# A four-layer forward and backward pass: where the upper weights are transposed, how the lower pass gets its input, and the order of work at the borders

## The chip, the cores and the metric

The kernel runs on one NeuronCore of one Trainium2 chip. The metric is the device time of one execution in microseconds. The core has a matrix engine (TensorE, PE in the profile, with its weight loads as PEld), three engines for elementwise work (VectorE as DVE, ScalarE as ACT, GpSimd as POOL) and SyncE (SP), from whose queue this kernel issues its transfers to 16 DMA engines. SBUF is the on-chip memory with 128 partitions; PSUM, in 8 banks, takes the results of PE.

## The reference

Four residual layers A, B, A, B with the same weights in both pairs, on x of 2048 tokens by 512 features in bfloat16, each behind a layer norm without affine part; then the gradients of everything for a given gradient of the output.

```python
x = x + A(layernorm(x), wqkv, wo)               # layer 0
x = x + B(layernorm(x), w_gate, w_up, w_down)   # layer 1
x = x + A(layernorm(x), wqkv, wo)               # layer 2
x = x + B(layernorm(x), w_gate, w_up, w_down)   # layer 3
# A: linear attention, 32 heads of 16; phi(t) = where(t > 0, t + 1, exp(t)) + 1e-6
#    kv = sum_s phi(k) v;  z = sum_s phi(k);  o = (phi(q) kv) / (phi(q) z + 1e-6);  o @ wo
# B: (sigmoid(h @ w_gate) * (h @ w_up)) @ w_down, with an inner width F = 1376
out, vjp = jax.vjp(f, x, wqkv, wo, w_gate, w_up, w_down); return out, *vjp(grad_out)
```

## The kernel before

The tokens are cut into 16 tiles of 128 (`NST`), the 512 features into 4 chunks (`NDC`), the inner width into 11 chunks (`NFC`; the last has 96 columns, `FLAST`) and, for PSUM, into three slices of 512, 512 and 352 columns (`FSL`). The residual stream `xs` stays in SBUF in float32. "Upper" weights are w_gate, w_up and w_down of B, "lower" pass means the pass over a B layer that follows its A layer.

The forward work runs in two pairs of layers, 0 with 1 and 2 with 3. For each pair `kq_fwd` walks over the 16 tiles once: it forms the keys and queries (L616), takes the exponential on ACT (`e_t`, L633), clamps it on DVE (`a_t`, L636), joins both to phi (`pk_all`, `pq_all`, L639), stores phi of the query (`sv_phq`, L642) and gathers X, the sum of h transposed times phi(k) (L624). In layer 0 the tile `a_t`, which the clamp writes and the store reads, comes from a pool of three; the forward weights are loaded behind the phq stores of tiles 2, 5, 8 and 11. The queries of the last two tiles are left over (`late_q`); their phi steps are the list `phis`. After the walk, `kq_fwd` makes the small matrix M (L793) and its transpose (L802), and the first tiles of the attention output.

`ab_fwd` is the lower pass. For tile `st` (a step) it does the gate and up products in three slices (`gu`, L922), the sigmoid and its complement on ACT (L924, L926), their product with u on DVE and POOL (`hh_t` at L929, `ssd_t` at L930), and, one or two steps later, the down product (`finish`, L956), which waits for `hhT`, the transpose of `hh_t`. For tiles 2 to 14 (`HH_DMA`) that transpose is one DMA (`dma_T`, L949); for 0, 1 and 15 PE transposes blocks (`t_tp`, L941) and ACT copies them (L944, L946). Beside it the attention output of a later tile passes through `front1` (den), `front2` (`pqnstage`, L863), `front3` (transposes at L374 and the copy to `pqnT`) and `attn_y` (L884, with the residual add at L892 and the statistics at L449 to L455). `ln.apply(st + 2)` then writes the normed `hstage` on ACT (L460), and `ln.stage_T` turns it with four PE transposes (`ln_tp`, L374) and a copy (L381 on DVE or L383 on ACT) into `hT`, the stationary operand of the gate and up products.

The border is the stretch between the two functions: the end of `kq_fwd` (M, attention of tiles 0 and 1, the late phi steps) and steps 0 and 1 of `ab_fwd`, in which nothing but a fixed hand-written order fills PE.

The order of PE, ACT, DVE and POOL in the forward part is as written (a manual schedule). SP is not in it: transfers go out as the program issues them, and a transfer that waits for its data holds those behind it.

The backward pass over B needs the upper weights transposed. `wT_units` makes them during the first pair: nine pieces, each one DMA transpose (two where the last 96 rows of a chunk are left) from the input into a staging tile `wt_st`, and a store from there into DRAM (`wdT_d`, `wuT_d`, `wgT_d`). Two pieces are issued ahead of the border, the others at the even steps of layer 1. `b_weight_loads` loads the three results into the resident tiles at steps 2, 5 and 8 of layer 3, and again for layer 1. The backward passes (`b_bwd_p1`, with `dhh_mm` at L1110, `transposes` at L1209 and L1211 and the product at L1252; `a_bwd_p1`; the weight gradients at L1495 and L1511) follow.

Of the kernel before, what the change touches and what calls it, by code (L numbers as in the profile page):

```python
# [18 lines left out]
D = 512  # L19
# [41 lines left out]
def kernel(  # L61
# [64 lines left out]
    )  # L126
    k.dwp = dict(
# [11 lines left out]
    with tc.tile_pool(name="wfwd", bufs=1, reuse_waits="tile") as wfwd, ExitStack() as lctx, tc.manual_schedule(engines=EM):  # L139
# [25 lines left out]
        def load_wd():  # L165
# [14 lines left out]
            hT=lctx.enter_context(tc.tile_pool(name="ln_hT", bufs=4, reuse_waits="tile")),  # L180
# [3 lines left out]
        with tc.tile_pool(name="aq0", bufs=1, reuse_waits="tile") as aq:  # L184
            A = kq_fwd(k, aq, 0, lns[0], lns[1], x_bf)
            with tc.tile_pool(name="wt_stage", bufs=2, reuse_waits="tile") as wt_stage:
                piece, flush = wT_units(k, wt_stage, B_w_gate, B_w_up, B_w_down)
                piece()
                piece()
                A.tail()  # L190
                ab_fwd(k, A, lns[1], {**{st: piece for st in range(0, 14, 2)}, NST - 2: flush}, nxt=lns[2])
        xctx.close()
        with tc.tile_pool(name="aq2", bufs=1, reuse_waits="tile") as aq:
# [4 lines left out]
            def b_weight_loads():  # L198
                def wd():
                    k.wdT = wb.tile([P, NDC, F], BF16, name="wdT", tag="w_c")  # L200
                    nc.sync.dma_start(out=k.wdT[:], in_=k.wT["wdT"].rearrange("(c p) f -> p c f", p=P))

                def wx(nm, tag):
                    t = wb.tile([P, NFC, D], BF16, name=nm, tag=tag)
                    setattr(k, nm, t)
                    nc.sync.dma_start(out=t[:, 0:NFC - 1, :],
                                      in_=k.wT[nm][0:(NFC - 1) * P, :].rearrange("(c p) j -> p c j", p=P))
                    nc.sync.dma_start(out=t[0:FLAST, NFC - 1, :], in_=k.wT[nm][(NFC - 1) * P:F, :])
                return wd, lambda: wx("wuT", "w_a"), lambda: wx("wgT", "w_b")
# [20 lines left out]
            def last_cb(i):  # L230
# [3 lines left out]
                else:  # L234
                    k.pre["dd"] = pre.tile([P, 2, F], BF16, name="pre_dd")
                    for fs in range(2):
                        dd_ops(k, k.pre["dd"], k.pre["ssd"], fs, dhh_mm(k, k.pre["gT"], fs))
            A.tail()
            ab_fwd(k, A, lns[3], dict(zip((2, 5, 8), b_weight_loads())), out_cb=out_cb, last_cb=last_cb)
# [5 lines left out]
    if True:  # L245
        def load_b_weights():
            wd, wu, wg = b_weight_loads()
            wd()
            wu()
            with tc.issue_after(k.hold):  # L250
                wg()
# [117 lines left out]
def transpose_blocks(k, ps_pool, dst, src_blocks, evac, tag="tp"):  # L369
# [1536 lines left out]
```

## Time and profile before

| | us |
|---|---|
| median of 3 runs | 1136.25 (1135.55 to 1138.84) |
| the profiled execution | 1135.02, span 1133.3 |
| PE busy | 1109.4 (98%) |
| DVE, ACT, POOL busy | 706.9, 484.2, 291.2 |
| DMA, mean over the 16 engines | 90.3% of the span |

Where PE stands by stage (busy us of PE in each stretch, granted clock, share of DMA):

| stretch, us | what runs | PE busy | clock | DMA |
|---|---|---|---|---|
| 18 to 59 | `kq_fwd`, layer 0 | 39.10 of 41 | 1.00 | 0.92 |
| 59 to 88 | border to layer 1, steps 0 to 2 | 22.86 of 29 | 1.00 | 0.70 |
| 88 to 232 | rest of layer 1, walk of layer 2 | 143.30 of 144 | 1.00 | 0.97 |
| 246 to 280 | border to layer 3 | 27.88 of 34 | 1.00 | 0.46 |
| 280 to 398 | rest of layer 3 | 118.00 of 118 | 1.00 | 0.91 |
| 398 to 1133 | backward | 731.10 of 735 | 1.00 | 0.94 |

How to read it: a line of the work list has the start, the duration, the engine, the program line, the operation, output<-input by the program's names, shapes and count; in brackets stands how long the engine had been idle before, and what ended that. The duration of a group of pipelined products reaches into the next group. SPq is SP issuing a transfer, not the transfer itself.

### The profile page before, as it was taken

How to read it: one execution, taken by the hardware profiler on the slowest of the kernel's cores; microseconds unless marked ns; L12 is line 12 of the kernel's file. 1: busy time of each engine (PE TensorE's matmuls, PEld its weight loads, DVE VectorE, ACT ScalarE, POOL GpSimd, SP SyncE). 2: the span in 40 equal slices, each digit the busy share in tenths (PEclk: the TensorE clock that was granted, in tenths of full speed). 3: DMA queues.
4: the chain of work that ended last, by engine and by line, in shares of the span. 5: the costliest groups of instructions: out<-in, count | busy, mean ns of one | idle time of the engine just before them, and what ended most of it. 6: DMA issues, size and time to landing. Idle time of an engine off the chain costs nothing.

```text
span 1133.3 us, 20011 instructions
## 1 busy us (share of the span) xinstructions
PE 1109.4 (98%) x7468; PEld 648.8 (57%) x7468; DVE 706.9 (62%) x1344; ACT 484.2 (43%) x909; POOL 291.2 (26%) x518
## 2 busy tenths in 40 slices
PE   8979999998999999999999999999999999999998
PEld 4444554444555555554456468855546745448888
DVE  6788886778776456664975850166664976852211
ACT  6676666555756543433625431224324515410000
POOL 5647776435666400000110220000000110210000
PEclk9999999999999999999999999999999999999999
DMA  8967999855899999997899997799998899969996
GB/s 270 309 197 212 273 282 283 245 142 183 223 294 265 269 261 262 302 255 207 222 244 313 220 260 237 195 283 289 257 283 260 205 282 289 241 194 298 263 205 192
DMA packets 413682, 282.36 MB, mean 249 GB/s; under 512 B 198608, under 2 KB 399504, under 8 KB 409744
## 3 DMA queue, kind: packets, MB, share of 16 engines
q1 hardware_dynamic: 412432, 280.03, 90.3%
q8 instruction: 58, 0.95, 0.3%
q10 hardware_dynamic: 1152, 1.05, 0.3%
q14 instruction: 40, 0.33, 0.1%
HBM read 125.44 MB, written 115.70 MB: 213 GB/s over the span
## 4 chain that ended last, share of the span: by engine, by line
PE 89%; DVE 6%; DMA 3%; ACT 1%; issue 1%; POOL 0%; DVEq 0%; SPq 0%; POOLq 0%
PE p_ps L1511 18%; PE dh_ps L1252 13%; PE dh_ps L1756 7%; PE p_ps L1495 7%; PE y_ps L956 6%; PE dhh_ps L1110 6%; PE g_ps L922 6%; PE u_ps L922 6%; PE T_ps L1209 3%; PE dpk_ps L1791 2%; PE GT_ps L1652 2%; PE dp_ps L1624 2%; PE y_ps L884 2%; PE t_mm L616 2%; PE X_ps L624 2%; PE t_ps L374 1%
## 5 line engine op out<-in xcount | busy, mean ns | idle before, releaser
L1511 PE MATMUL p_ps<-p_set,p_a 128*128 128x256 bf16 (+1 forms) x2032 | 210.1, 264 | 0.0
L1511 PEld LDWEIGHTS <-p_a 128*128 128x128 bf16 x2048 | 185.9, 98 | 22.2
L1132 DVE TENSOR_TENSOR dd<-dhh_ps,ssd 128x512 bf16<-128x512 f32 x144 | 82.4, 629 | 121.3 <-PE dhh_ps L1110 117.4
L930 POOL TENSOR_TENSOR ssd_t<-hh_t,oms 128x512 bf16<-128x512 bf16 (+1 forms) x96 | 100.7, 1060 | 50.1 <-ACT out_t L226 13.5
L1252 PEld LDWEIGHTS <-ddT 128*128 128x128 bf16 (+1 forms) x704 | 67.6, 98 | 74.6 <-DMA ddT<-dd 2.4
L922 PEld LDWEIGHTS <-hT 128*128 128x128 bf16 x768 | 72.5, 98 | 65.2 <-DVE hT L381 1.4
L1084 POOL TENSOR_SCALAR ab<-c 128x2 f32<-128x2 f32 x64 | 12.4, 194 | 377.9 <-DVE junk L1081 364.7
L1211 ACT COPY ddT<-T_ps 128x1024 bf16<-128x1024 bf16 (+1 forms) x72 | 58.8, 819 | 115.2 <-PE T_ps L1209 62.0
L1076 ACT ACTIVATE t_sb<-dh_ps,rstd_all 128x512 f32<-128x512 f32 x64 | 44.0, 688 | 115.7 <-issue 65.0
L922 PE MATMUL g_ps<-wg,hT 128*128 128x512 bf16 (+1 forms) x384 | 90.0, 357 | 0.4 <-DVE hT L381 0.4
L924 ACT ACTIVATE ssd_t<-g_ps 128x512 bf16<-128x512 f32 (+1 forms) x96 | 53.4, 556 | 86.1 <-PE g_ps L922 80.3
L922 PE MATMUL u_ps<-wu,hT 128*128 128x512 bf16 (+1 forms) x384 | 90.0, 357 | 0.0
L1485 DVE TENSOR_TENSOR dw_stg<-p_ps,dw_stg 128x512 bf16<-128x512 f32 (+3 forms) x43 | 28.1, 653 | 98.1 <-PE p_ps L1511 81.4
L929 DVE TENSOR_TENSOR hh_t<-u_ps,ssd_t 128x512 bf16<-128x512 f32 (+1 forms) x96 | 60.4, 631 | 44.0 <-PE u_ps L922 34.2
L1252 PE MATMUL dh_ps<-wgT,ddT 128*128 128x512 bf16 (+1 forms) x352 | 85.2, 379 | 0.0
L1252 PE MATMUL dh_ps<-wuT,ddT 128*128 128x512 bf16 (+1 forms) x352 | 81.3, 379 | 0.8 <-DMA ddT<-dd 0.7
L956 PE MATMUL y_ps<-wd,hhT 128*128 128x512 bf16 (+1 forms) x352 | 81.3, 379 | 0.6 <-DVE x L958 0.6
L1495 PE MATMUL p_ps<-p_a,p_set 128*128 128x512 bf16 (+1 forms) x352 | 81.2, 379 | 0.0
L1110 PE MATMUL dhh_ps<-wdT,gTb 128*128 128x512 bf16 x336 | 74.2, 357 | 0.0
L956 PEld LDWEIGHTS <-hhT 128*128 128x128 bf16 (+1 forms) x352 | 34.2, 98 | 41.1 <-issue 0.7
L1081 DVE SCALAR_TENSOR_TENSOR junk<-t_sb,h_ld 128x512 bf16<-128x512 f32 x48 | 37.2, 774 | 28.9 <-ACT t_sb L1076 23.7
L926 ACT ACTIVATE oms<-g_ps 128x512 bf16<-128x512 f32 (+1 forms) x96 | 52.8, 550 | 3.9 <-POOL ssd_t L930 3.7
(227 smaller groups left out, 1824.2 us busy)
## 6 DMA issues: line engine op xcount, KB each, us to landing
p_set<-sv_hdd SPq DMA_DIRECT2D x30, 1024.0 KB, 6.2
sv_ssd<-ssd_t SPq DMA_DIRECT2D x32, 688.0 KB, 4.2
ssd<-sv_ssd SPq DMA_DIRECT2D x24, 688.0 KB, 5.1
sv_hdd<-dd SPq DMA_DIRECT2D x24, 512.0 KB, 5.0
sv_hdd<-hh_t SPq DMA_DIRECT2D x32, 320.0 KB, 4.4
p_a<-sv_h SPq DMA_DIRECT2D x16, 512.0 KB, 6.5
p_set<-sv_dqk SPq DMA_DIRECT2D x8, 1024.0 KB, 7.5
h_ld<-sv_h SPq DMA_DIRECT2D x24, 256.0 KB, 4.7
```

What stands on the lines that cost most here:

```text
L922: nc.tensor.matmul(ps[:, 0:w], lhsT=hT[:, kc, :], rhs=w_sb[:, kc, c0:c0 + w], start=(kc == 0), stop=(kc == NDC - 1))
L924: nc.scalar.activation(ssd_t[:, 0, c0:c0 + w], g_ps[:, 0:w], ACT.Sigmoid)
L929: nc.vector.tensor_tensor(hh_t[:, c0:c0 + w], u_ps[:, 0:w], ssd_t[:, 0, c0:c0 + w], ALU.mult)
L930: nc.gpsimd.tensor_tensor(ssd_t[:, 1, c0:c0 + w], hh_t[:, c0:c0 + w], oms[:, 0:w], ALU.mult)
L956: nc.tensor.matmul(y_ps[:], lhsT=T["hhT"][0:r, fc, :], rhs=k.wd[0:r, fc, :], start=(fc == 0), stop=(fc == NFC - 1))
L1110: k.nc.tensor.matmul(ps[:, 0:w], lhsT=gT[:, jc, :], rhs=k.wdT[:, jc, c0:c0 + w], start=(jc == 0), stop=(jc == NDC - 1))
L1132: k.nc.vector.tensor_tensor(dd_part(dd, a, fs), ps[:, 0:w], ssd[:, a, c0:c0 + w], ALU.mult)
L1211: nc.scalar.copy(out[:, :, 0:nfull, :], tps[:, :, 0:nfull, :])
L1252: nc.tensor.matmul(T["dh"][:], lhsT=T["ddT"][0:r, dd_block(a, fc), :], rhs=(k.wuT, k.wgT)[a][0:r, fc, :], start=(i == 0), stop=(i == 2 * N ...
L1495: nc.tensor.matmul(ps[0:r, :], lhsT=set_t[:, st, c * P:c * P + r], rhs=self.ops[j["l"], "g"][:, st, :], start=(st == 0), stop=(st == NST - 1))
L1511: nc.tensor.matmul(ps[:, icl * w:(icl + 1) * w], lhsT=self.ops[j["l"], "h"][:, st, ic * P:(ic + 1) * P], rhs=set_t[:, st, 0:w], start=(st ...
L1756: nc.tensor.matmul(dh_ps[:], lhsT=lhsT, rhs=rhs, start=(i == 0), stop=(i == len(ops) - 1))
```

## The change

- *Upper weights.* `wT_units` and its staging are gone from the first pair. In the second pair the same pieces are transposed straight into the resident tiles (`k.bw`): four ahead of the border, two, two and one after the stores of steps 0, 1 and 2. The last chunk is transposed as the last 128 columns, overlapping the one before, and its first 32 rows are set to zero (`zero_rows`, step 6). At steps 7, 9 and 11 the resident tiles are stored to DRAM, from where layer 1's backward pass loads them with one transfer each.
- *Input of the lower pass.* In layer 1 the `hT` of tiles 3 to 15 is made by a DMA transpose of `hstage`, issued after `ln.apply` two steps ahead of its use. Layer 3 keeps PE transposes. The pools of `hT` and `pqnT` lose one buffer each.
- *Borders* (both pairs). 24 and 14 transposes of the identity go into a PSUM tile as filler; the first `hT` copy goes to ACT; the late phi of the last tile gets its own tile and moves into step 0; in steps 0 and 1 the order of the transposes, `attn_y` and `ln.apply` is another.
- *Layer 0.* `a_t` has four buffers.
- *Backward pass over B.* The last chunk is treated like the others, with 128 rows, in `transposes` (one copy in place of two) and in the product with wuT and wgT.

```diff
-            hT=lctx.enter_context(tc.tile_pool(name="ln_hT", bufs=4, reuse_waits="tile")),
+            hT=lctx.enter_context(tc.tile_pool(name="ln_hT", bufs=3, reuse_waits="tile")),
...
-                piece, flush = wT_units(k, wt_stage, B_w_gate, B_w_up, B_w_down)
-                piece()
-                piece()
-                A.tail()
-                ab_fwd(k, A, lns[1], {**{st: piece for st in range(0, 14, 2)}, NST - 2: flush}, nxt=lns[2])
+            A.tail()
+            ab_fwd(k, A, lns[1], {}, nxt=lns[2])
...
+            def by_cols(f0, w):
+                def load():
+                    t = k.bw["wdT"] if f0 else b_tile("wdT")
+                    nc.sync.dma_start(out=t[:, :, f0:f0 + w], in_=B_w_down[f0:f0 + w, :], transpose=True)
+                return load
+
+            def by_rows(src, nm, c0, n):
+                def load():
+                    t = k.bw[nm] if c0 else b_tile(nm)
+                    nc.sync.dma_start(out=t[:, c0:c0 + n, :], in_=src[:, c0 * P:(c0 + n) * P], transpose=True)
+                    if c0 + n == NFC - 1:
+                        nc.sync.dma_start(out=t[:, NFC - 1, :], in_=src[:, F - P:F], transpose=True)
+                return load
+
+            def zero_rows():
+                for nm in ("wuT", "wgT"):
+                    nc.gpsimd.memset(k.bw[nm][0:P - FLAST, NFC - 1, :], 0.0)
...
+            parts = [(0, 4), (4, 3), (7, 3)]
+            pieces = [by_cols(f0, w) for f0, w in FSL]
+            pieces += [by_rows(B_w_up, "wuT", *p) for p in parts] + [by_rows(B_w_gate, "wgT", *p) for p in parts]
...
+            some()
+            some()
             A.tail()
-            ab_fwd(k, A, lns[3], dict(zip((2, 5, 8), b_weight_loads())), out_cb=out_cb, last_cb=last_cb)
+            side = {**{st: some for st in range(3)}, 6: zero_rows}
+            side.update(zip((7, 9, 11), [b_store(nm) for nm in ("wdT", "wuT", "wgT")]))
+            ab_fwd(k, A, lns[3], side, out_cb=out_cb, last_cb=last_cb)
...
+def keep_busy(k, ps, n):
+    for i in range(n):
+        k.nc.tensor.transpose(ps[:, 4 + i % 4, :], k.ident[:], k.ident[:])
...
+    def dma_T(self, st):
+        self.hTs[st] = hT = self.k.lnres["hT"].tile([P, NDC, P], BF16, name="hT")
+        self.k.nc.sync.dma_start(out=hT[:], in_=self.hs.pop(st), transpose=True)
...
-                        work.tile([P, 2, D], BF16, name="a_t", bufs=3)[:, 1, :])
+                        work.tile([P, 2, D], BF16, name="a_t", bufs=4)[:, 1, :])
...
+            if st == NST - 1:
+                e_t = a_t = aq.tile([P, D], BF16, name="lq_t")[:]
...
+        ln_ps = k.ps["ln"].tile([P, 8, P], BF16, name="ln_tp", tag="ln_tp")
+        keep_busy(k, ln_ps, 24)
         for jc in range(NDC):
             nc.scalar.copy(MT_sb[:, jc, :], mt_ps[jc][:])
...
         A.front3(1, "g", "vector")
         phis[0]()
-        A.ln.stage_T(0)
-        phis[1]()
+        keep_busy(k, ln_ps, 14)
+        A.ln.stage_T(0, "scalar", ln_ps)
+        A.late_phi = phis[1]
         A.attn_mm(1)
...
+HT_DMA = {1: range(3, NST), 3: ()}
...
-        pqnT = pool.tile([P, NDC, P], BF16, name="pqnT", bufs=3)
+        pqnT = pool.tile([P, NDC, P], BF16, name="pqnT", bufs=2)
...
-                ln.stage_T(st + 1, "scalar")
+                if st + 1 not in HT_DMA[l]:
+                    ln.stage_T(st + 1, "scalar")
...
                 gu(T, hT, 1)
+                A.late_phi()
                 ln.apply(1)
...
                 A.front1(FLAG)
+                transposes(T, 0)
                 A.attn_y(2)
-                transposes(T, 0)
                 A.front2(FLAG)
...
-                if st == 1:
-                    A.attn_y(FLAG)
-                else:
+                if st > 1:
                     ln.stage_T(st + 1)
                 A.front1(st + FLAG)
                 gu(T, hT, 2)
                 if st == 1:
+                    A.attn_y(FLAG)
                     ln.stage_T(2)
...
             if st > 0:
+                if st == 1:
+                    transposes(T, 2)
                 ln.apply(st + YLAG)
+                if st + YLAG in HT_DMA[l]:
+                    ln.dma_T(st + YLAG)
...
-            out = ddT[:, 2 * fcs[0]:2 * (fcs[-1] + 1), :].rearrange("p (a n) t -> p a n t", a=2)
-            nc.scalar.copy(out[:, :, 0:nfull, :], tps[:, :, 0:nfull, :])
-            if nfull < len(fcs):
-                nc.scalar.copy(out[0:FLAST, :, nfull, :], tps[0:FLAST, :, nfull, :])
+            nc.scalar.copy(out, tps[:, :, 0:n, :])
```

More of the change, by code (lines that the diff above doesn't have):

```diff
@@ L700, in kq_fwd @@
                 e_t = work.tile([P, 2, D], BF16, name="e_t", bufs=2)
-                a_t = work.tile([P, 2, D], BF16, name="a_t", bufs=3)
+                a_t = work.tile([P, 2, D], BF16, name="a_t", bufs=4)
                 ek, ak, eq, aqt = e_t[:, 0, :], a_t[:, 0, :], e_t[:, 1, :], a_t[:, 1, :]
@@ L1202, in transposes @@
             fcs = fchunks_of_slice(fs)
-            nfull = len([fc for fc in fcs if fc_rows(fc) == P])
+            n, w = len(fcs), FSL[fs][1]
             tps = ps_tile(k, "t", [P, 2, 4, P], BF16, "T_ps")
```

103 lines of the change are left out of this document (34 added, 69 removed).

## The prediction

> **What bounds the kernel now.** I read the page's totals first, then the list of PE's work in order of time, then the same list for a steady step of the lower forward pass, then the DMA groups.
>
> ```profile
> PE 1109.4 (98%) x7468; PEld 648.8 (57%) x7468; DVE 706.9 (62%) x1344; ACT 484.2 (43%) x909; POOL 291.2 (26%) x518
> ...
> PEclk9999999999999999999999999999999999999999
> ```
>
> PE is busy for 1109.4 of 1133.3 us and its granted clock is full in every slice. So a change pays only where it takes work from PE or closes one of the gaps that add up to 23.9 us; relief of ACT, DVE or SP is worth nothing by itself. The gaps lie where the change works. PE's groups with an idle time before them (in brackets, with what ended it), from 48 us to the fourth step of the first lower pass:
>
> ```profile
> 48.52 1.02 PE L616 MATMUL y_mm<-wqkv,hTst 128*128 128x512 bf16 x4 [1.73 <-DVE pk_all L639]
> ...
> 65.30 0.40 PE L374 MATMUL g_ps<-ident,pqnstage 128*128 128x128 bf16 x4 [1.62 <-DVE pqnstage L863]
> ...
> 66.93 0.40 PE L374 MATMUL ln_tp<-ident,hstage 128*128 128x128 bf16 x4 [1.23 <-ACT hstage L460]
> ...
> 68.39 1.04 PE L922 MATMUL g_ps<-wg,hT 128*128 128x512 bf16 x4 [0.21 <-DVE hT L381]
> ...
> 72.97 0.40 PE L374 MATMUL t_ps<-ident,pqnstage 128*128 128x128 bf16 x4 [0.95 <-DVE pqnstage L863]
> ...
> 76.55 0.33 PE L941 MATMUL t_tp<-ident,hh_t 128*128 128x128 bf16 x3 [0.45 <-ACT hhT L944]
> ...
> 81.51 1.04 PE L884 MATMUL y_ps<-M_sb,pqnT 128*128 128x512 bf16 x4 [0.73 <-ACT pqnT L383]
> ...
> 86.97 0.40 PE L374 MATMUL ln_tp<-ident,pqnstage 128*128 128x128 bf16 x4 [0.41 <-DVE pqnstage L863]
> ```
>
> The reader should see one gap of 1.73 at 48.52 and seven at the border from layer 0 to 1, 5.60 us together (0.49 more lies at 59.82 and 60.42). The border from layer 2 to 3 has the same gaps from 250.80 to 277.94, within 0.01 us each. What keeps DVE at the first gap, and at the border:
>
> ```profile
> 47.25 0.49 DVE L636 TENSOR_SCALAR a_t<-e_t 128x512 bf16<-128x512 bf16 x1 [2.71 <-DMA sv_phq<-a_t]
> ...
> 68.26 0.28 DVE L636 TENSOR_SCALAR a_t<-e_t 128x512 bf16<-128x512 bf16 x1
> 68.57 0.69 DVE L639 SCALAR_TENSOR_TENSOR pq_all<-t_mm,a_t 128x512 bf16<-128x512 f32 x1
> 69.18 0.68 DVE L892 TENSOR_TENSOR x<-y_ps,x_bf 128x512 f32<-128x512 f32 x1
> ```
>
> A steady step of the lower pass, 8.336 us from one y_ps group to the next (104.66, 112.99, 121.33):
>
> ```profile
> 118.66 0.81 ACT L460 ACTIVATE hstage<-x,ln_nmr,rstd_all 128x512 bf16<-128x512 f32 x1
> ...
> 119.47 2.37 SPq L949 DMA_TRANSPOSE hhT<-hh_t  x1
> ...
> 125.27 0.39 PE L374 MATMUL ln_tp<-ident,hstage 128*128 128x128 bf16 x4
> ...
> 125.50 0.76 PE L922 MATMUL g_ps<-wg,hT 128*128 128x352 bf16 x4
> ...
> 125.69 0.59 ACT L383 COPY hT<-ln_tp 128x512 bf16<-128x512 bf16 x1
> ```
>
> PE gives 125.50 - 125.27 = 0.23 us of each step to turning hstage into hT; the copy at 125.69 feeds the next step's first product. The DMA groups that price the replacement (median us to landing last):
>
> ```profile
> hhT<-hh_t SPq DMA_TRANSPOSE x26, 4.2
> ...
> dq_ld<-sv_dqk SPq DMA_TRANSPOSE x24, 4.0
> ...
> dq_ld<-sv_dqk SPq DMA_DIRECT2D x8, 128.0 KB, 4.7
> ```
>
> **The change, part by part.** (1) *hT by DMA in layer 1, tiles 3 to 15.* Removed: 13 x 0.225 = 2.93 us of PE, and 13 ACT copies of 0.586 off PE's path. Added: 13 DMA transposes of 128 KB on SP, ahead of the stores of ssd and hh_t. In the step above the hstage of the tile two ahead ends 0.89 us into the step (119.47 against 118.58, where its first gate product starts), and its hT is needed at the start of the next step, 8.11 us in (8.336 less 0.225). On SP an hhT is issued ahead of it in most steps, 1.44 to 2.6 us in this pass; landing then takes, by the other transposes, 3.5 to 6.7 us, median 4.2 to 4.5. So hT is there 0.89 + 1.44 + 4.4 = 6.7 us in, 1.4 to spare. Not so for tile 4: step 3 has no y_ps of the lower layer and lasts only 5.96 us, so hT lands at 95.80 + 0.81 + 1.4 + (3.5 to 4.4) = 101.5 to 102.4, and would be needed at 101.67 - 0.23 = 101.4: a stall of 0.1 to 1.0. Tiles 7, 11 and 15 stand behind a 512 KB store of h (landing 3.8 by itself). I take 0.6 lost in all and -2.3; ends -2.9 (no stall) and +12 (late in each step, rival A). What hides the DMA itself is the room that the weights leave: DMA is busy 0.97 of 88 to 232 us, and the nine weight transposes (SP issues of 1.2 to 3.4 us each) and eleven stores leave this pass. SP's stores behind a waiting hT hold no tile that PE needs within a step. [...]
>
> (2) *Weights.* No weight transposes in layer 1's pass: PE was dense there, gain 0. In the second pair, four pieces are issued about 246 to 257 us and five up to step 2, SP issues of 1.2 to 3.4, in a stretch where DMA is busy 0.46; the three stores of 1.4 MB at steps 7, 9 and 11 stand for three loads of 1.3 to 1.4 MB at 2, 5 and 8, behind which an hhT took 9.3 us to land and PE did not wait (PE busy 118.00 of 118.00 us, 280 to 398). Cost 0; ends -0.3 and +5 (rival D). One load in place of two for the lower layer, and two memsets on POOL: 0.
>
> (3) *a_t with four buffers.* The clamp at 47.25 waited 2.71 us for the store of three tiles back, issued at 37.62, right behind the 1.4 MB load of wu (35.72), and landed 9.5 later. With four it waits for the store issued at 35.34, ahead of that load. DVE is then ready earlier than ACT's e_t lets it be, so part of the 1.73 stays: I put y_mm at 47.4 rather than 48.52, -1.1; ends 0 and -1.73. Layer 2's pass has its own tiles: 0.
>
> (4) *Borders.* The filler, 24 and 14 transposes of 56 ns (eight take 0.44 us) = 1.34 and 0.79 us, goes into gaps of 1.62 and 1.23: cost 0, and with the clock full already, gain 0. The late phi (0.28 + 0.69 us at 68.26) leaves DVE's row of work between y_ps(1) and pqnstage(2), which ends the gap at 72.97; the first hT copy moves from DVE (0.41, queued behind a clamp and phi until 67.92) to ACT (0.59). Walking the queues by hand: the first gate product 0.4 earlier (68.0), the pqnstage(2) transposes at 72.0, step 1 at 75.5 instead of 76.7, the first finish at 82.8 instead of 84.0, the ln_tp at 86.97 at 85.4. That is 1.5 per border of 5.6 to gain, at most 3.5 that these queues could free, at least 0: -3.0 for two, ends 0 and -7.0. What is late next is DVE again, by the residual add and statistics of tile 2.
>
> (5) *ddT with whole rows.* Twelve blocks as before; six transposes of 96 columns took 0.34 and eight of 128 take 0.44, the same 56 ns; products with 96 rows 381 ns against 379; one ACT copy in place of two of 0.577 and 0.374, off the path: 0.
>
> Sum: -2.3 - 1.1 - 3.0 = -6.4. The profiled execution took 1135.02 us (span 1133.3 and 1.7 around it), so 1128.6; the median, 1136.25, lies 1.2 above the profiled one, and I forecast it at 1129.8.
>
> **The rivals.** *A, hT late (slower).* Place: the first gate product of each step of layer 1. It decides from a landing of about 8.11 - 0.89 - 1.44 = 5.8 us on. For it: the largest hhT landing in this pass is 6.7, one of 9.3 stood behind a weight load, and SP's issue of hhT reached 2.6. Against: the medians 4.2 to 4.5, and that the weight traffic leaves. At 6.7 each step is 0.93 longer, 13 x 0.93 = +12 in place of -2.3: 1135.0 - 1.1 - 3.0 + 12 = 1143, on the median's scale 1144; half the tiles late gives 1137. [...] *B, the border's order gives nothing.* DVE's own work there, not the order, sets the gaps (24.67 of 29 us busy, 59 to 88): only (1) and (3), 1132.8. *C, the borders close further.* 3.5 us each: 1125.8. *D, the weights jam the second border.* Layer 3's first hhT copy waits for the stores of M and X, about 4 us before they matter; behind four transposes with up to 8.5 us of issue they can come 5 us too late: 1134.8.
>
> **How the numbers follow.** Forecast 0.56, A 0.14 (half of it above 1140), B 0.13, C 0.10, D 0.07. A measurement of this kernel can tell about 0.3%, 3.4 us, from no change: faster is below 1132.8, slower above 1139.7. Faster: forecast, C and half of B: 0.70, cut to 0.66 for the forecast's own tail. Slower: A's upper part and what I haven't seen: 0.13. Same: 0.21. The likeliest one's own range is 1127 to 1132.5 (hT -1.5 to -2.9, a_t 0 to -1.7, borders -1 to -2.3 each); with C below, and D, B and half of A above, 1125 to 1139.
>
> **What would show it.** Right: step of the first lower pass 8.11 us, no ln_tp there after tile 2, hT landing under 5.5 us, first gate products with no wait on a DMA but at tile 4; y_mm's gap at 48.52 under 0.7; the two borders about 1.5 shorter each, the filler within the gaps; 280 to 398 still dense. Wrong: a wait of PE for hT in most steps (A), border gaps of the same sum at other places (B), an ACT copy waiting for a store near 262 us (D).

## The result, and the profile after

The changed kernel took 1128.79 us (median of 6 executions, 1127.65 to 1130.32) against 1136.6 us of the kernel before beside it; the ratio of the means is 0.9929, with a 95% interval from 0.9913 to 0.9946, so 8.1 us less (7.8 by the medians). Measured again on another chip it took 1129.06 against 1135.17, ratio 0.995 (0.9934 to 0.9966), 5.7 us less (6.1 by the medians). The forecast was 1129.8, or 6.4 less. The profiled execution took 1129.17 (span 1127.5), 5.85 below that of before.

From the page of the changed kernel, its totals and the granted clock:

```profile
PE 1110.7 (99%) x7492; PEld 650.3 (58%) x7492; DVE 709.2 (63%) x1342; ACT 475.0 (42%) x866; POOL 292.8 (26%) x520
...
PEclk9999999999999999999999999999999999999999
```

PE's busy time rose by 1.3 us although it lost 2.9 us of hT transposes, because the filler counts as work (groups of 1.50 and 0.94 us at the first border). What fell is the idle time, from 23.9 to 16.8 us. Of these 7.1 us some 4.2 are filler that stands where PE was idle before (1.33 and 0.78 us in the two gaps of each border) and gain no time by themselves (what they do for the clock is shown with e4); the other 2.9, and the 2.9 of transposes, make the 5.8. PE's groups with idle time before them, from the border to the fourth step of the first lower pass (the gap at 48.52 is gone altogether):

```profile
63.25 0.40 PE L408 MATMUL g_ps<-ident,pqnstage 128*128 128x128 bf16 x4 [0.29 <-DVE pqnstage L860]
...
64.88 0.40 PE L408 MATMUL ln_tp<-ident,hstage 128*128 128x128 bf16 x4 [0.45 <-ACT hstage L445]
...
69.98 0.40 PE L408 MATMUL t_ps<-ident,pqnstage 128*128 128x128 bf16 x4 [0.39 <-DVE pqnstage L860]
...
73.50 0.34 PE L938 MATMUL t_tp<-ident,hh_t 128*128 128x128 bf16 x3 [0.38 <-DVE hh_t L926]
...
79.26 1.04 PE L881 MATMUL y_ps<-M_sb,pqnT 128*128 128x512 bf16 x4 [0.26 <-ACT pqnT L417]
81.27 2.54 PE L953 MATMUL y_ps<-wd,hhT 128*128 128x512 bf16 x11 [0.26 <-DVE x L889]
...
100.61 1.04 PE L881 MATMUL y_ps<-M_sb,pqnT 128*128 128x512 bf16 x4 [0.92 <-ACT pqnT L417]
```

The gaps of 1.62 and 1.23 are now filler with 0.29 and 0.45 left; 0.95 became 0.39, 0.73 became 0.26, 0.41 went. New is 0.92 at 100.61. For hT there is a single wait in layer 1, of 0.2 us by PE's weight load at tile 11, which makes one step 8.33. In the lower pass ACT copies no hT after tile 2, and the DMA row of the new transposes has the median landing of 3.8 us (2.6 to 5.7 over the two profiles of this kernel):

```profile
hT<-hstage SPq DMA_TRANSPOSE x13, 3.8
```

A steady step is 8.11 us, as forecast (y_ps groups at 109.60, 117.71, 125.82). The places where the time went, as start times of the same PE group in both traces (the key product and the first ln_tp are the ends of the walk):

| place | before | after | shift | gained since the line above |
|---|---|---|---|---|
| key product of the walk, near 18 us | 18.50 | 18.34 | -0.16 | |
| first ln_tp of the border to layer 1 | 59.82 | 57.77 | -2.05 | 1.89 |
| y_ps of tile 1, layer 1 | 89.97 | 86.55 | -3.42 | 1.37 |
| last y_ps of layer 1 | 203.52 | 198.27 | -5.25 | 1.83 |
| first ln_tp of the border to layer 3 | 250.80 | 245.44 | -5.36 | 0.11 |
| y_ps of tile 1, layer 3 | 280.93 | 274.22 | -6.71 | 1.35 |
| last y_ps but one of layer 3 | 390.71 | 383.99 | -6.72 | 0.01 |
| end of the span | 1133.3 | 1127.5 | -5.8 | -0.9 |

The 0.9 given back in the backward pass holds a wait for a ddT transpose of 1.51 us at 828.61, where before had 0.74 at 850.67. Such waits differ from one execution to the next (before's other profile 0.84, the changed kernel's other one 1.70, one run below 3.3 in two waits); by the other two profiles the backward pass gives back 0.5 (741.8 to 742.3 us from the last y_ps but one to the end). Part (5) of the change works there and was not undone by itself, nor were the smaller pools of `hT` and `pqnT`, nor the place of the weights without the DMA transposes of hT.

### The profile page after: what moved, and what is told of

The parts are those of the page before. It is cut to its first block, busy times and chain, and to the rows that moved or that the text cites. A ratio compares the mean times of both kernels' runs of the same rounds, so it can differ in the third digit from the quotient of the medians.

```text
span 1127.5 us, 20018 instructions
## 1 busy us (share of the span) xinstructions
PE 1110.7 (99%) x7492; PEld 650.3 (58%) x7492; DVE 709.2 (63%) x1342; ACT 475.0 (42%) x866; POOL 292.8 (26%) x520
## 3 DMA queue, kind: packets, MB, share of 16 engines
q10 hardware_dynamic: 1152, 1.05, 0.3%
## 4 chain that ended last, share of the span: by engine, by line
PE 76%; DVE 2%; DMA 2%; ACT 1%; issue 1%; SPq 0%; POOL 0%
PE p_ps L1511 18%; PE dh_ps L1251 12%; PE dh_ps L1756 7%; PE p_ps L1495 6%; PE dhh_ps L1112 6%; PE y_ps L953 3%; PE g_ps L919 3%; PE u_ps L919 3%; PE dpk_ps L1791 2%; PE GT_ps L1652 2%; PE dp_ps L1624 2%; PE T_ps L1211 2%; PE t_mm L606 1%; DMA ddT<-dd 1%; PE X_ps L614 1%; PE y_ps L881 1%
## 5 line engine op out<-in xcount | busy, mean ns | idle before, releaser
L1213 ACT COPY ddT<-T_ps 128x1024 bf16<-128x1024 bf16 (+1 forms) x72 | 65.5, 913 | 116.9 <-PE T_ps L1211 65.2
L1251 PEld LDWEIGHTS <-ddT 128*128 128x128 bf16 x704 | 67.4, 98 | 75.8 <-DMA ddT<-dd 3.9
L1251 PE MATMUL dh_ps<-wgT,ddT 128*128 128x512 bf16 x352 | 85.1, 379 | 0.0
L1251 PE MATMUL dh_ps<-wuT,ddT 128*128 128x512 bf16 x352 | 81.2, 379 | 1.6 <-DMA ddT<-dd 1.5
```

The costliest lines, as they stand in the source:

```text
L1213: nc.scalar.copy(out, tps[:, :, 0:n, :])
L1251: nc.tensor.matmul(T["dh"][:], lhsT=T["ddT"][:, dd_block(a, fc), :], rhs=k.bw[("wuT", "wgT")[a]][:, fc, :], start=(i == 0), stop=(i == 2 * ...
```

## The experiments

Each kernel was run beside the kernel before. "Undone" means taken out of the changed kernel.

| run | what | median, us | ratio to before (95%) |
|---|---|---|---|
| r_after_again | the changed kernel | 1129.06 | 0.995 (0.9934 to 0.9966) |
| e1_hT_by_PE | hT by DMA undone | 1132.43 | 0.9978 (0.9968 to 0.9988) |
| e2_a_t_three | fourth a_t buffer undone | 1130.89 | 0.9966 (0.9953 to 0.9978) |
| e3_border_as_before | borders undone | 1133.61 | 0.998 (0.9971 to 0.999) |
| e4_no_filler | filler undone | 1130.91 | 0.9963 (0.995 to 0.9976) |
| e5_weights_first_pair | weights' staging undone | 1143.89 | 1.0077 (1.0061 to 1.0093) |
| e12_weights_odd_steps | the same, pieces at odd steps | 1140.31 | 1.0042 (1.0027 to 1.0058) |
| e8_hT_dma_both | hT by DMA in layer 3 too | 1135.81 | 1.0009 (0.9999 to 1.002) |
| e10_before_filler | before, with the filler alone | 1135.93 | 1.0009 (0.9998 to 1.002) |
| e9a_order | two orders altered | 1130.7 | 0.9948 (0.9929 to 0.9967) |
| e11_order_six | the same, hT by DMA for six tiles of layer 3 | 1129.35 | 0.9941 (0.9924 to 0.9957) |

Before had medians of 1135.34 (beside e1 to e4), 1135.17 (beside r_after_again, e5, e10, e8) and 1135.64 (beside the others). A difference of 1 us between rows is not told by these intervals; below, terms are read from PE groups in the traces, which repeat to about 0.1 us where no DMA is late (the first border took 28.78 or 28.79 us in after, in r_after_again and in e1, from the first ln_tp to the y_ps of tile 1).

**The changed kernel again.**

> The changed kernel itself, for comparison on the chip of the runs so far, where before took 1135.3. If the terms add up (hT 1.8, a_t 1.7, borders 2.7, a full clock in each execution about 0.6 at the median), it takes 1128.5 to 1129 here too, and what was undone singly cost more than its term for another reason; if this chip gives a smaller gain, 1129.5 to 1130.5, the single undoings (1130.9, 1130.9, 1132.4, 1133.6) stand at their terms. Granted clock 1.00 in every execution either way.

It took 1129.06, and the clock was 1.00 in all six executions, as in the six of the first measurement. Against this median (before's stood at 1135.3 beside the first four runs and 1135.2 here, on two chips) the single undoings cost 3.4 (e1), 1.8 (e2), 4.6 (e3) and 1.9 (e4), together more than the whole change brings; the traces say which part of each is the term.

**hT by PE again.**

```diff
-HT_DMA = {1: range(3, NST), 3: ()}
+HT_DMA = {1: (), 3: ()}
```

> The changed kernel with hT of layer 1 made by PE and an ACT copy again in all 16 tiles; the rest of the change stays. Theory (the DMA transposes pay by PE's time alone, less two stalls): steps of the first lower pass 8.34 us instead of 8.11; 13 x 0.225 = 2.9 us more PE work, and the waits of 0.92 (at the step of tile 4) and 0.21 (tile 11) go, so +1.8 us against the changed kernel, about 1130.6; the end of the second lower pass 1.8 later, nothing else moves. Rival (the copies taken from ACT also free the border or the next walk): more than +2.9. Rival (DMA transposes cost elsewhere what PE saves): within 0.5 us of the changed kernel.

Layer 1, from the y_ps of tile 1 to its last one, took 113.98 us (87.73 to 201.71) against 111.72 of the changed kernel: 2.26, between the theory's 1.8 and the 2.9 at which the first rival begins. It is 2.93 less the 0.21 and less 0.43, since half of the new wait at tile 4 is there without any DMA (0.49 at 101.81). The borders and the next walk are as long as in the changed kernel to 0.01 us (28.79, 28.78 and 47.17), so nothing else moved. The rest of the 3.4 is not hT's in the profiled execution: its walk began 1.16 later, behind a load of wqkv that PE awaited for 1.49. Whether the other executions began late too is not known, so by the times alone the rival's "more than 2.9" is not ruled out.

**Three a_t buffers.**

```diff
-                        work.tile([P, 2, D], BF16, name="a_t", bufs=4)[:, 1, :])
+                        work.tile([P, 2, D], BF16, name="a_t", bufs=3)[:, 1, :])
...
-                a_t = work.tile([P, 2, D], BF16, name="a_t", bufs=4)
+                a_t = work.tile([P, 2, D], BF16, name="a_t", bufs=3)
```

> The changed kernel with three a_t buffers. Theory (the fourth buffer alone removes the wait for the store behind the load of wu): one gap of 1.7 us before the key product near 48 us comes back, with a clamp waiting for sv_phq, everything after it 1.7 later, 1130.5. Rival (the start 0.16 us earlier and the DMA order of this run did it): no gap or a smaller one, 1128.8 to 1129.3.

The clamp waits for the store again, and PE has gaps in that stretch:

```profile
45.72 0.77 DVE L626 TENSOR_SCALAR a_t<-e_t 128x512 bf16<-128x512 bf16 x1 [1.20 <-DMA sv_phq<-a_t]
```

```profile
47.27 1.02 PE L606 MATMUL y_mm<-wqkv,hTst 128*128 128x512 bf16 x4 [0.50 <-DVE pk_all L629]
...
51.10 1.02 PE L606 MATMUL t_mm<-wqkv,hTst 128*128 128x512 bf16 x4 [0.22 <-DVE pk_all L629]
```

The gap came back, smaller, and the walk from the key product near 18 us to the border is 1.05 us longer than in the changed kernel (40.48 against 39.43): 0.72 in two parts here, 0.71 in e10, 1.73 in both profiles of the kernel before. It goes with when the store behind the load of wu lands, which was 9.5 us after its issue in the profile shown before the prediction, 8.2 in e10 and 8.0 here. In the changed kernel that store landed as late as ever (9.4 us), and with four buffers no clamp waited for it; so the buffer closed the gap, and not an earlier start or another order of transfers, the rival here. The fourth buffer is worth 1 to 1.9 us, and with it no such gap was seen in any run.

**The borders as before.**

```diff
-        ln_ps = k.ps["ln"].tile([P, 8, P], BF16, name="ln_tp", tag="ln_tp")
-        keep_busy(k, ln_ps, 24)
...
-        keep_busy(k, ln_ps, 14)
-        A.ln.stage_T(0, "scalar", ln_ps)
-        A.late_phi = phis[1]
+        A.ln.stage_T(0)
+        phis[1]()
...
-                transposes(T, 0)
                 A.attn_y(2)
+                transposes(T, 0)
...
-                if st > 1:
+                if st == 1:
+                    A.attn_y(FLAG)
+                else:
                     ln.stage_T(st + 1)
...
-                if st == 1:
-                    transposes(T, 2)
                 ln.apply(st + YLAG)
```

> The changed kernel with both borders in the order of before: no filler, first hT copy on DVE, late phi ahead of step 0, old order in steps 0 and 1. Theory: from the first ln_tp of the border to the y_ps of step 2 each border is 1.35 us longer, gaps of 1.6 and 1.2 and 0.9 come back, 1128.8 + 2.7 = 1131.5. Rival (what stands in the way is DVE's work, and the a_t buffer or the absent weight pieces shortened the borders): within 0.7 us of the changed kernel.

The borders took 30.31 and 30.25 us, against 28.78 and 28.78, and before's 30.15 and 30.13. The theory holds with 3.0 in place of 2.7, although no weight pieces and four a_t buffers stand around them; "DVE's work, not its order" falls. Some of the 0.3 beyond 2.7 can be the clock, which drops to a half for 3.4 us behind the gaps of both borders here and was full in before's profile. In this trace the start adds 0.5 and layer 3 0.7 (0.55 of it a wait for one hhT), and layer 1 takes 0.6 back; the rest of the 4.6 is not in it.

**Without the filler.**

```diff
-        keep_busy(k, ln_ps, 24)
...
-        keep_busy(k, ln_ps, 14)
```

> The changed kernel without the 38 filler transposes at each border. Theory (they fill idle time, the clock is full either way): 0, within 0.3 us in the trace; the gaps of 1.62 and 1.23 come back at the same places and the products behind them start and last as before. Rival (the filler keeps something of PE fast): products behind the gaps longer, or the two borders later by 0.5 us or more each. Rival (the filler costs): borders 0.2 to 1 us shorter without it.

My theory fell. All five executions had a mean clock of 0.997 or 0.998 instead of 1.00, and the borders took 29.17 and 29.60 us against 28.78. PE's groups behind the gaps; a gate group of four takes 1.03 at the full clock:

```profile
63.24 0.40 PE L408 MATMUL g_ps<-ident,pqnstage 128*128 128x128 bf16 x4 [1.63 <-DVE pqnstage L858]
...
64.86 0.40 PE L408 MATMUL ln_tp<-ident,hstage 128*128 128x128 bf16 x4 [1.23 <-ACT hstage L445]
65.31 1.19 PE L879 MATMUL y_ps<-M_sb,pqnT 128*128 128x512 bf16 x3
66.29 1.91 PE L917 MATMUL g_ps<-wg,hT 128*128 128x512 bf16 x4
68.00 1.54 PE L917 MATMUL u_ps<-wu,hT 128*128 128x512 bf16 x4
69.37 1.03 PE L917 MATMUL g_ps<-wg,hT 128*128 128x512 bf16 x4
```

Four gate products take 1.91 us for 1.03: the clock is at a half from 65.6 to 69.0. The view by stretches has it at 0.50 (columns: the stretch, its length, busy time of PE, PEld, DVE, ACT, POOL, the granted clock, the DMA share, GB/s):

```profile
64.00:66.00 2.00, 1.08 (x7) 0.60 (x9) 1.91 (x3) 1.39 (x2) 1.07 (x1) 0.90 0.93 320
66.00:68.00 2.00, 2.00 (x7) 0.64 (x5) 1.39 (x3) 0.00 (x0) 0.00 (x0) 0.50 0.40 139
68.00:70.00 2.00, 2.00 (x8) 0.84 (x7) 1.86 (x6) 1.09 (x2) 0.82 (x2) 0.74 0.00 0
70.00:72.00 2.00, 2.00 (x15) 1.18 (x14) 1.52 (x4) 1.56 (x3) 0.97 (x1) 1.00 0.00 0
```

The two borders lose 1.2 us by it in the trace. Part of the slow stretch is absorbed: the wait of 0.39 for pqnstage behind it is gone. By the medians it is 1.9, but the intervals overlap.

**The kernel before, profiled again.** Unchanged.

> The kernel before once more, for a profile. In most executions on these chips its mean granted clock was 0.997 to 0.998, in the profile shown 1.00. If that is what the gaps of the border do, the clock in this profile, if below 1.00, drops to about 0.5 for some 3 us right behind the gap of 1.23 at one border or both, and the border is no more than 0.5 us longer than the 30.15 (first ln_tp to the y_ps of tile 1) that it takes with the full clock, since DVE sets its pace. Rival: the drop lies elsewhere.

This execution had a mean clock of 0.997, and the drop begins within the second of the two gaps of the first border (at 65.83 us) and lasts beyond it (same columns as above):

```profile
66.00:68.00 2.00, 1.14 (x6) 0.81 (x8) 1.97 (x4) 0.58 (x1) 0.85 (x1) 0.50 1.01 343
68.00:70.00 2.00, 2.00 (x6) 0.65 (x5) 1.92 (x5) 0.00 (x0) 0.00 (x0) 0.50 0.48 164
70.00:72.00 2.00, 2.00 (x6) 0.76 (x5) 1.86 (x6) 1.08 (x2) 0.81 (x2) 0.50 0.96 175
72.00:74.00 2.00, 2.00 (x9) 0.85 (x8) 1.30 (x3) 0.52 (x2) 0.52 (x1) 0.83 0.96 194
```

The border took 31.57 us (59.54 to 91.11) instead of 30.15, so the drop cost 1.4, not the 0.5 at most that I expected; the second border kept the full clock and took 30.13. Of the 59 executions of before in these three measurements 44 had a mean clock below 1.00; in each of the three their median is 1.0 to 1.6 us above that of the others (1135.62 against 1134.58, 1135.19 against 1134.06, 1135.69 against 1134.07; the others are 10, 2 and 3). The gaps don't tell the two profiles of before apart: in both they are 1.62 and 1.23 us with 0.40 of work between them, and the clock stayed at 1.00 in one and fell to 0.50 in the other.

What goes with a drop can be worked out from the clock that the traces record. In each of the fourteen profiles all changes of the clock lie on one grid of 3.41 us, and a half clock lasts one window of it (e3, e4, e5, e8, e12) or two (6.83 us here, from 65.83 to 72.66). Adding up the time without PE work in every window at full clock, from the first one to 30 us before the end: nine windows have 2.04 us or more, and each is followed by a half clock; all others have 2.02 or less, and none is. The borders of before stand on both sides of that line:

| profile of before | window, us | PE busy in it | without PE work | the next window |
|---|---|---|---|---|
| here | 62.42 to 65.83 | 1.37 | 2.04 | half clock |
| the one ahead of the prediction | 62.25 to 65.67 | 1.79 | 1.63 | full |
| the same | 65.67 to 69.08 | 1.98 | 1.43 | full |

The gaps are the same, but here the windows begin 0.45 us later against them, and more of both falls into one. That the line lies near 2.0 us is what these fourteen traces show, no more, and that the time without PE work in such a window is what brings the drop is my reading of them.

**Before with the filler alone.**

```diff
+        ln_ps = k.ps["ln"].tile([P, 8, P], BF16, name="ln_tp", tag="ln_tp")
+        keep_busy(k, ln_ps, 24)
         for jc in range(NDC):
             nc.scalar.copy(MT_sb[:, jc, :], mt_ps[jc][:])
...
         phis[0]()
+        keep_busy(k, ln_ps, 14)
         A.ln.stage_T(0)
```

> The kernel before with only the 24 and 14 filler transposes added at each border. Theory (gaps of 1.6 and 1.2 us behind each other can lower the granted clock for some 3 us, and the filler prevents it): clock 1.00 in every execution, where 14 of 24 executions of before show 0.997 to 0.998; time 0.5 to 1 us below before's median, since the slow stretch is half hidden behind DVE. Rival (the lower clock comes from elsewhere in the pass): the share of executions below 1.00 stays near a half, time within 0.3. Rival (the filler delays the border): 0.5 to 2 us above before.

The clock was 1.00 in 11 of 12 executions (before, beside it: 2 of 23), so the filler does what it is for in the old order too. The borders took 30.13 and 30.12 in its trace, as in before with the full clock: the filler doesn't delay them. Yet the median is 0.8 above before's, ratio 1.0009 with an interval that holds 1. The trace's forward part ends 0.8 earlier than before's (last y_ps but one at 389.90 against 390.71), and its backward pass has two waits for ddT of 1.86 and 1.46. That the filler gains time in the kernel before is not shown: its full clock should bring it to the 1134.1 to 1134.6 of before's executions with the full clock, and it stands above them.

**Weights back in the first pair.** `wT_units` as in before (the last chunk stored with its 32 zero rows), two pieces ahead of the border, seven at even steps; loads at steps 2, 5, 8 of layer 3.

```diff
-            A.tail()
-            ab_fwd(k, A, lns[1], {}, nxt=lns[2])
+            with tc.tile_pool(name="wt_stage", bufs=2, reuse_waits="tile") as wt_stage:
+                piece, flush = wT_units(k, wt_stage, B_w_gate, B_w_up, B_w_down)
+                piece()
+                piece()
+                A.tail()
+                ab_fwd(k, A, lns[1], {**{st: piece for st in range(0, 14, 2)}, NST - 2: flush}, nxt=lns[2])
...
-            side = {**{st: some for st in range(3)}, 6: zero_rows}
-            side.update(zip((7, 9, 11), [b_store(nm) for nm in ("wdT", "wuT", "wgT")]))
+            side = {st: (lambda nm=nm: b_load(nm)) for st, nm in ((2, "wdT"), (5, "wuT"), (8, "wgT"))}
```

> The changed kernel with the weights' transposes, their staging and stores back in the first pair, and loads at steps 2, 5 and 8 of layer 3; everything else as changed. Theory (hT has slack whatever else is in the queue): hT lands in 3.5 to 5.5 us, waits of PE for hT under 1.5 us together in layer 1, total within 1 us of the changed kernel. Rival (taking the weights out of layer 1's pass is what lets hT come in time): hT stands behind transposes that take SP up to 3.4 us to issue; landing plus queue over 5.8 us at five tiles or more, waits for hT of 3 to 8 us together, total 3 to 8 us above the changed kernel.

It is the largest effect of all, 14.8 us above the changed kernel and slower than before, beyond what the rival expected, though hT is late at three tiles (7, 11 and 15) and not at five or more. PE waits for hT three times, 10.35 us together:

```profile
126.97 1.04 PE L962 MATMUL g_ps<-wg,hT 128*128 128x512 bf16 x3 [2.84 <-DMA hT<-hstage]
...
163.49 1.89 PE L962 MATMUL g_ps<-wg,hT 128*128 128x512 bf16 x4 [3.61 <-DMA hT<-hstage]
...
200.37 1.27 PE L962 MATMUL g_ps<-wg,hT 128*128 128x512 bf16 x4 [3.90 <-DMA hT<-hstage]
```

Behind the longer two the clock falls as well (0.83 from 160 to 170 us, 0.81 from 197 to 206), and layer 1 is 14.3 us longer than in the changed kernel (126.0 us). But no transfer of hT was slow: landing was 2.6 to 5.0 us, median 3.6, no more than in the changed kernel. What was late is the issue. SP's queue ahead of the first of the three:

```profile
115.88 3.18 SPq L431 DMA_TRANSPOSE wt_st<-in_B_w_up_dram  x1
119.10 0.58 SPq L436 DMA_DIRECT2D wuT_d<-wt_st  x1
119.80 1.99 SPq L989 DMA_TRANSPOSE hhT<-hh_t  x1
121.88 1.00 SPq L515 DMA_DIRECT2D sv_h<-hstage  x1
122.94 1.92 SPq L529 DMA_TRANSPOSE hT<-hstage  x1
```

One piece holds SP for 3.2 us, hhT, the store of h and hT follow without a pause, and hT lands 4.0 us behind its issue, at 126.97. Its hstage had been ready since 116.75. In the changed kernel the same hT is issued at 118.03:

```profile
115.76 1.38 SPq L946 DMA_TRANSPOSE hhT<-hh_t  x1
117.24 0.74 SPq L472 DMA_DIRECT2D sv_h<-hstage  x1
118.03 1.69 SPq L486 DMA_TRANSPOSE hT<-hstage  x1
```

**The pieces at odd steps** (the edit is against the run above).

```diff
-                ab_fwd(k, A, lns[1], {**{st: piece for st in range(0, 14, 2)}, NST - 2: flush}, nxt=lns[2])
+                ab_fwd(k, A, lns[1], {**{st: piece for st in range(1, 14, 2)}, NST - 2: flush}, nxt=lns[2])
```

> The kernel with the weights in the first pair again, but with the pieces at the odd steps 1, 3, ... 13 of layer 1 and not at the even ones. Same traffic, another order on SP: at the even steps a piece stands ahead of hhT, the store of h and hT of tiles 7, 11 and 15. Theory (what makes hT late is SP's queue ahead of it, about 7 us from the piece to hT, and not the transfer): with the pieces at odd steps hT of those tiles is issued in time; waits of PE for hT fall from 10.4 us to under 2.5, total 1129 to 1132.5. Rival (the DMA engines' load, or the transposes of weights as such): waits for hT still 6 us or more, at whichever tiles, total 1138 or more.

The number goes against the theory, and both signs of the rival came true (6 us or more, 1138 or more): waits for hT of 1.03, 1.93, 0.90, 1.75 and 1.24, together 6.9, and one of 4.16 for an hhT, whose issue alone took 4.5:

```profile
158.95 1.04 PE L962 MATMUL g_ps<-wg,hT 128*128 128x512 bf16 x4 [1.93 <-DMA hT<-hstage]
...
168.13 1.04 PE L962 MATMUL g_ps<-wg,hT 128*128 128x512 bf16 x4 [0.90 <-DMA hT<-hstage]
...
206.75 4.01 PE L996 MATMUL y_ps<-wd,hhT 128*128 128x512 bf16 x10 [4.16 <-DMA hhT<-hh_t]
```

The place of the pieces beside the store of h is thus not the whole cause: moving them gave back 3.6 of the 14.8 us. The likeliest rest is how much SP has to issue. Again no landing was long (3.0 to 5.3 us, median 3.8); the hT that PE awaits until 168.13 had its hstage at 157.76 and was issued at 163.94, behind a piece of 3.65 that began at 157.99. Adding up SP's rows of the trace over the rest of the lower pass:

| kernel, stretch | SP issuing, us | share |
|---|---|---|
| before, layer 1, 92 to 208 | 98.8 (weights 23.8) | 0.85 |
| changed, layer 1, 88 to 200 | 84.0 (hT 19.2) | 0.75 |
| e5, layer 1, 89 to 215 | 112.0 (weights 25.9, hT 21.5) | 0.89 |
| e12, layer 1, 88 to 212 | 109.9 (weights 24.8, hT 22.0) | 0.89 |
| changed, layer 3, 276 to 392 | 93.0 | 0.80 |
| e8, layer 3, 275 to 392 | 108.9 (hT 27.0) | 0.93 |

In e5 the issues sum to 112 us, as much as the whole pass of 112 us in the changed kernel: at the changed kernel's pace SP's queue would have no room left. That this sum is the cause is argued, not shown, for an issue has no fixed price. In layer 1 of e5 an hhT held SP for 1.4 us at the median, but in its layer 3 one held it for 5.71, 3 us behind the load of a weight of 1.4 MB (5.26 at the same place of before):

```profile
323.78 1.19 SPq L230 DMA_DIRECT2D wuT<-wuT_d  x1
325.07 0.98 SPq L907 DMA_DIRECT2D sv_pqn<-pqnstage  x1
326.15 0.52 SPq L249 DMA_DIRECT2D out_dram<-out_t  x1
326.78 5.71 SPq L989 DMA_TRANSPOSE hhT<-hh_t  x1
```

So an issue may hold time that comes from transfers still under way; that it does is not shown, and the rival of e12, the load of the DMA engines, stays open. Their share from 88 to 200 us is 0.98 in e5 and 1.04 in e12, 0.89 in the changed kernel; hhT's issue, 18.8 us for 13 in the changed kernel, is 21.8 and 23.6 in the two. The share alone doesn't tell it either: it is 0.75 in e1, with 20.5 us for the 13.

**hT by DMA in layer 3 too.**

```diff
-HT_DMA = {1: range(3, NST), 3: ()}
+HT_DMA = {1: range(3, NST), 3: range(3, NST)}
```

> The changed kernel with hT by DMA in layer 3 too, tiles 3 to 15. Theory (13 x 0.225 = 2.9 us of PE less what comes late): steps of the second lower pass 8.11, less a wait of about 0.9 behind the short step 3 and 0.5 to 1.5 at the three tiles whose hT stands behind a 1.4 MB store: 0.5 to 1.8 us below the changed kernel. Rival (the weight traffic of layer 3 makes hT late, which would be why layer 3 keeps PE): waits for hT of 3 us or more in steps 1 to 3 and 7 to 11, total no better than the changed kernel or up to 3 us worse.

The rival holds, and more: 6.8 us above the changed kernel, with a mean clock below 1.00 in 8 of 12 executions. The steps are 8.11 from 292 to 349 us, as they should be, but PE waits 2.67 us for hT at 288.19 and 1.84 at 373.98, 1.22 for a copy to pqnT, and in the first steps of the backward pass 1.40 and 0.96. SP's rows ahead of the first of these, a stretch without a pause again, of which the two gate pieces take 4.07:

```profile
275.69 4.07 SPq L213 DMA_TRANSPOSE wgT<-in_B_w_gate_dram  x2
279.86 0.53 SPq L864 DMA_DIRECT2D sv_pqn<-pqnstage  x1
280.43 0.47 SPq L237 DMA_DIRECT2D pre_ssd<-sv_ssd  x1
281.00 1.57 SPq L946 DMA_TRANSPOSE hhT<-hh_t  x1
282.67 3.42 SPq L486 DMA_TRANSPOSE hT<-hstage  x1
```

**Two orders altered, and six tiles of layer 3.** In e9a the transpose of hT goes out ahead of the store of h, and in step 3 the copy to pqnT goes ahead of the norm on ACT; e11 adds hT by DMA for tiles 6 to 11 of layer 3.

```diff
+        if st in HT_DMA[l]:
+            self.dma_T(st)
         if st % NB == NB - 1:
             nc.sync.dma_start(out=dram_batch(k.sv[l]["h"], st // NB), in_=self.cur[:])
...
+                if st == 3:
+                    A.front3(st + FLAG, "t")
                 ln.apply(st + YLAG)
-                if st + YLAG in HT_DMA[l]:
-                    ln.dma_T(st + YLAG)
...
-            if st > 0:
+            if st > 0 and st != 3:
                 A.front3(st + FLAG, "t" if st in by_dma else "ln")
```

```diff
-HT_DMA = {1: range(3, NST), 3: ()}
+HT_DMA = {1: range(3, NST), 3: range(6, 12)}
```

> The changed kernel with two orders altered: hT's transpose is issued ahead of the 512 KB store of h instead of behind it, and in step 3 the copy to pqnT goes ahead of the norm of tile 5 on ACT. Theory: the wait of 0.92 near 100 us and that of 0.21 at tile 11 go, 1.1 us shorter, about 1128.0. Rival (DVE or hT takes the wait's place within the short step 3): 0.3 or less.

> The same, and hT by DMA also for tiles 6 to 11 of layer 3, that is after the last weight transposes and (but for the first two) before the stores of 1.4 MB. Theory: six steps of 8.11 instead of 8.34, no wait for hT, 6 x 0.225 = 1.35 us below the run of the altered order alone, 1126.7. Rival (any DMA transpose in layer 3 meets the stores at steps 7 and 9): waits of 1 us or more for hT, gain gone.

Neither reached its forecast: the medians are 1130.7 and 1129.35 instead of 1128.0 and 1126.7. In e9a layer 1 is 110.77 us (86.66 to 197.43), 0.95 less than in the changed kernel; both waits are gone (one of 0.20 is new at 107.25), so the 0.92 was the norm ahead of the copy on ACT, not hT. In e11 five steps of layer 3 are 8.11 and one 8.13. But layer 3, from the y_ps of tile 1 to the last but one, took it back in each, with 111.91 us in e9a and 110.37 in e11 against 109.77. First e9a's wait, then e11's:

```profile
385.29 2.55 PE L955 MATMUL y_ps<-wd,hhT 128*128 128x512 bf16 x11 [1.21 <-DMA hhT<-hh_t]
```

```profile
377.79 2.55 PE L955 MATMUL y_ps<-wd,hhT 128*128 128x512 bf16 x11 [1.14 <-DMA hhT<-hh_t]
```

Such a wait for hhT late in layer 3 stands in five of the nine profiles of kernels that store the weights at steps 7 to 11 of layer 3 (0.43 in e4, 0.55 in e2 and e3, and these two), but in neither of the two of the changed kernel; why it comes in some is open. Neither version is told apart from the changed kernel by its time.

## Why the prediction came out

- *What bounds the kernel* held: 6.7 us of PE gaps and transposes went from the forward part, and the time followed, less what the backward pass gave back. That the sum, -6.4, came within 0.6 of the profiled -5.85 is in part luck: (3) brought 0.8 more than its term, (1) 0.5 and (4) 0.3 less, and 0.9 came from a pass that the sum left out.
- *(1) hT by DMA*, -2.3: -1.83 in the trace. The mechanism (13 x 0.225 less a stall at tile 4) held, and the stall was sized well, but for a wrong reason: hT of tile 4 came in time, if only just (landed at 97.57, 3.4 us after its issue, and first used at 97.81), and PE awaited a copy to pqnT that stood behind a norm on ACT, which e9a showed by turning the two round. So hT made no stall at tile 4, and the 0.92 there was a wait for the copy. The one wait for hT itself was 0.2, at tile 11, behind the store of h as foreseen; one landing took 5.7, above the 5.5 named as a sign. Half of the new wait at tile 4 is there without the DMA too (0.49 in e1), and why is open.
- *Rival A*, hT late: it is real, but the step "it decides from a landing of about 5.8 us on" named the wrong quantity. In e5 and e12 landing stayed at 5.3 us or less, and PE waited 10.4 and 6.9 us: what was late was the issue (122.94 for an hstage ready at 116.75 in e5, 163.94 for one ready at 157.76 in e12). The price at which I put what stands ahead of hT on SP, 1.44 to 2.6 us of another transpose, leaves out a weight piece in the queue, which alone held SP for 3.18 and 3.65 there.
- *(2) Weights*, gain 0: true of PE in the kernel before, and of the table above, in which layer 3 shows no cost. Its stores late in layer 3 do seem to cost something in some executions, waits for hhT of 0.4 to 1.2 in five of nine profiles. But taken with (1) it is the part that matters most: undoing it alone costs 14.8 us. I had named the cover ("the room that the weights leave") without its price.
- *(3) a_t*, -1.1: -1.9 against the profiled execution, whose gap of 1.73 closed wholly. The reason why I left 0.6 of it was that ACT's e_t would be late: DVE does wait for it next, 1.18 us at 48.25, but no gap of PE follows. In other executions the gaps there to close were only 0.7.
- *(4) Borders*, -1.5 each: -1.37 and -1.35, by the path that was walked: counted from the start of the border, the first gate product and the transposes of pqnstage(2) came within 0.03 us of the forecast, the first finish 0.5 later than forecast, held for 0.26 by DVE's residual add. Undone, they return to 30.3. The step that failed is "with the clock full already, gain 0" for the filler: it rested on one profiled execution. In 44 of 59 others the mean clock was below 1.00, and without the filler the new order loses 1.2 us at its borders. It may also be part of the difference between the forecast's 6.4 and the first measurement's 8.1, since the sum was made against an execution with the full clock; that is not shown, as the clock of the executions beside the first measurement is not on record, and the second measurement gave 5.7.
- *(5) Whole rows*, 0: one copy of 0.789 us in place of 0.577 and 0.374, and PE's groups as before; nothing of it on the path; no run undid it alone.
- *The other rivals and the chances.* The gaps of the borders closed (against B), by 1.4 and not 3.5 each (against C), and the second border is as short as the first (against D). In the chances for "faster", forecast, C and half of B add up to 0.725 and not to 0.70.

## What to carry to other kernels

A queue that issues transfers can be filled like an engine: add up its issue times over the stage, with the new transfers in it, before asking how fast one of them lands, and don't take the price of an issue as fixed (the 13 of hhT in layer 1 took 18.8 us in the changed kernel, 21.8 and 23.6 with the weight pieces in the queue); here a pass of 112 us held 84 us of issues with 12 of the 13 new transposes among them, and the longer one with the weight pieces held 112. One part of a change can be worth 2 us beside another and cost some 12 without it (layer 1 took 126.0 us in e5 and 113.6 in the kernel before), so ask of each part whose cover another one makes or takes away. And read the granted clock from several executions before calling filler work useless.

## What was not expected of the hardware

- Two gaps of PE of 1.62 and 1.23 us with 0.40 us of transposes between them were enough to bring the granted clock to 0.50, for 3.41 us at each border in e4 and for 6.83 us in one execution of before, and in other executions of the same kernel not at all. In these traces the drop came behind a window of 3.41 us with 2.04 us or more without PE work, and never behind one with 2.02 or less. With 38 transposes of the identity at each border the clock was 1.00 in all 12 executions of the changed kernel, in 10 of 12 of e1 and in 11 of 12 of e10; without them it was lower in all 5 of e4 and in 10 of 11 of e3. In e5, e8 and e12, where PE waits in the lower passes for up to 3.90, 2.67 and 4.16 us, it was lower with them too, in 6 of 6, 8 of 12 and 6 of 7.
- A DMA transpose of a weight piece of 128 to 512 KB held SP's queue for 1.2 to 4.1 us, and one of hT (128 KB) for 1.2 to 3.4, while plain stores of 320 to 688 KB took 0.3 to 1.5 in the passes of the table above. Size doesn't tell it: the store of hh_t's last 96 columns (`sv_hdl`, 24 KB), third behind two larger ones, took 1.05 to 1.39 at the median of each pass.
